# Which engine runs which small job, and when: re-sorting the first stage of a fused attention and feed-forward kernel

## The chip, the cores and the metric

The kernel runs on one core of one Trainium2 chip. Its time is the device time of one execution in microseconds (us). A core has five engines with a queue each: TensorE (PE) for matmuls, VectorE (DVE), ScalarE (ACT), GpSimd (POOL) and SyncE (SP), which here only issues DMAs. An engine works through its queue in order, so an instruction that waits holds up all that is queued behind it.

## The reference

Two blocks follow each other, all in float32:

```python
# q, k, v: (8, 8, 576, 64); tau = 0.02
scores = scale * q @ k.T                       # scale = 1/8
thresh = max(scores, -1) - tau
scores = where(scores >= thresh, scores, -1e9)
attn = exp(scores - max(scores, -1))
attn = attn / (sum(attn, -1) + 1e-9)
x = (attn @ v) transposed to (4608, 512)       # 8 sequences of 576 rows, 8 heads of 64
h = x @ w_in                                   # 512 -> 2048
g = where(h > 0, h, exp(min(h, 0)) - 1)
out = g @ w_out                                # 2048 -> 512
```

## The kernel before

**Attention.** The 64 heads are worked in 32 pairs (`pr`), four pairs to a sequence. The 576 query rows of a pair are cut into four blocks of 128 rows and a rest of 64 rows for each head, which makes five steps (`i` = 0 to 4; 4, called `NC`, is the rest of both heads). A step has two heads (`h` = 0, 1), the last one only one tile for both. A step goes through these jobs:

- `sc`: the scores, on PE, into PSUM;
- `max`: the row maximum, on DVE; `th`: the threshold from it, on POOL or DVE;
- `exp`: the exponential on ACT, and `mask`: compare with the threshold, multiply and sum, on DVE. For a head listed in `MASK_ACT` (`WIDE_ACT` in the second stage) both are ACT passes instead: a steep leaky step at the threshold and then the exponential with its row sum;
- `su` and `rec`: the row sum and its reciprocal, on DVE; `su` on ACT for steps in `SU_ACT`;
- `norm`: the weights times the reciprocal. On ACT if the step and head are in `ACT_NORM`, on DVE if in `NORM_DVE`, else on POOL;
- the weights are turned (transposed) for the product with v: either `part` and `put` (PE transposes into a PSUM tile `rt`, then copies to `wTa`/`wTb` by ACT, or by DVE if in `PUT_DVE`), or `turned` and `landed` (DVE transposes 32x32 blocks, SP writes them to DRAM, `there`, and fetches them back);
- `val` and `out`: the product with v on PE, and its copies out of PSUM by ACT.

Around the steps, q and k of each pair are loaded, turned on DVE (`prep`), q scaled (`scale`; on ACT if the pair is in `SCALE_ACT`, else on POOL) and two small copies made on POOL (`copy`).

**Feed-forward.** The weights come in 32 pieces, whose 64-bit form is converted by `rest`, `shift`, `add`, `sign` and `end` (`SHIFT_POOL` and `REST_POOL` name the pieces whose `shift` or `rest` runs on POOL). The first two chunks of 256 tokens are plain matmuls (`half`, lines 1085 and 1137) that fill PE between the early attention jobs; their ELU is done in three parts (`post`) by ACT, POOL and DVE, or without DVE for units in `ELU_ACT`. All later chunks use a fast scheme with seven products of quarter matrices for eight; the sums of weight blocks that it needs are made early, on POOL for those in `IN_POOL` and else on DVE (`in`), together with sums of `w_out` (tile `t`) on POOL.

**The order of the first stage.** `early_tasks` covers the first 45 steps (`n` = 0 to 44: nine pairs). Each job has a due time: a base time by its place plus an entry of the table `MOVED`. The jobs are emitted in order of due time, and each draws the jobs that it needs ahead of it (`do`, line 1282). So a due time decides only where it is earlier than that of all jobs that need it. There are two PSUM tiles for turns and products (`room_for`): the third `part` or `val` in a row forces the `put` or `out` of the first ahead of it.

PE is also given transposes of the identity that nobody reads: 22 in `start`, 16 as the job `idle` in step 0, and those of `IDLES`, where `(n, x, count)` puts `count` of them just ahead of part `x` of step `n`'s turn:

```python
if (n, x) in idles:
    spare.append(idles[n, x])
room_for("t", lambda: do(("put", n, x)))
```

**The second stage.** From pair 9 on (`JOINED`) the kernel works in a fixed rhythm, two wide score groups per pair between 56 feed-forward matmul quarters, written as an agenda of times (`at`), again with small offsets from `MOVED`; keys that begin with `j` belong to pair 9, the first wide pair, and those with `f` and `s` to all others. In pair 9 `finish_of` (line 1893) puts a normalization on ACT if it is in `WIDE_NORM`, else on POOL:

```python
at(t_sum + 0.25 + 0.75 * h, lambda h=h: (normalize_act if (pr, i, h) in WIDE_NORM else normalize_pool)(pr, i, h), f"norm{i}{h}")
```

In the same stage ACT copies the products of the feed-forward out of PSUM (lines 1673, 1720 and 1721), and POOL and DVE add them up (1678, 1681).

Lines to follow in the profile: L656 scores, L713 `max`, L717 and L729 `th`, L751 `exp`, L736 and L742 the two ACT passes, L758 `mask`, L766 and L703 `su`, L772 `rec`, L709, L692 and L697 `norm` on POOL, DVE and ACT, L775 all PE transposes, L791 `put`, L851 `turned`, L876 the write to `there`, L884 the fetch, L908 and L913 `val`, L1043 `out`, L1223 `in`, L1250 and L1253 the sums `t` and their DMA.

Of the kernel before, what the change touches and what calls it, by code (L numbers as in the profile page):

```python
# [18 lines left out]
ACT_NORM = {(1, 1), (2, 1), (4, 1), (6, 0), (8, 0), (8, 1), (10, 0), (11, 1), (12, 1), (14, 0), (14, 1), (15, 0), (15, 1),  # L19
 (16, 0), (17, 0), (18, 0), (18, 1), (21, 0), (21, 1), (23, 0), (23, 1), (26, 0), (28, 0), (29, 0), (30, 1), (31, 0), (35,  # L20
 0), (36, 1), (37, 0), (38, 1), (40, 0), (40, 1), (41, 1), (42, 1), (43, 0), (43, 1), (44, 0)}
IN_POOL = {(0, 1), (0, 2), (1, 1), (2, 0), (2, 1), (2, 2), (3, 0), (3, 2), (4, 0), (4, 1), (5, 0), (5, 1), (6, 0), (6, 2),
 (7, 2)}
SU_ACT = {3, 13, 15, 20, 23, 25, 26, 29, 30, 31, 32, 33, 34, 35, 37, 39, 44}
QK_PE = set()
MASK_ACT = {(0, 0), (0, 1), (1, 1), (2, 0), (7, 1), (8, 0), (9, 1), (12, 1), (13, 0), (14, 1), (15, 0), (15, 1), (17, 0),
 (20, 0), (20, 1), (21, 0), (21, 1), (22, 0), (23, 0), (24, 0), (25, 0), (25, 1), (26, 0), (26, 1), (27, 0), (27, 1), (28,
 0), (29, 0), (30, 0), (30, 1), (31, 0), (32, 0), (33, 0), (33, 1), (35, 0), (36, 1), (37, 0), (37, 1), (38, 0), (39, 0),
 (40, 0), (41, 0), (42, 0), (44, 0)}
SHIFT_POOL = {0, 1, 2, 3, 13, 16, 18, 20, 21, 23, 27, 28, 29, 31}  # L30
REST_POOL = {2, 3, 4, 5, 7, 8, 11, 12, 15, 16, 22, 27, 30, 31}
IDLES = {(2, 2, 2), (5, 0, 9), (6, 1, 3), (7, 0, 1), (7, 1, 1)}
ELU_ACT = {(1, 0), (1, 3), (1, 5)}
NORM_DVE = {(4, 0), (12, 0), (13, 0), (19, 0), (25, 0), (25, 1), (28, 1), (31, 1), (32, 0), (32, 1), (33, 1), (34, 0), (35,
 1), (38, 0)}
WIDE_ACT = {(9, 1, 0), (9, 2, 1), (9, 4, 0)}
WIDE_NORM = {(9, 1, 1), (9, 2, 0)}
SCALE_ACT = {3, 6, 7, 9}
SUM_POOL = {0, 3}
SPLIT = {(4, 10)}  # L40
PUT_DVE = {(0, 2), (6, 2), (12, 0), (12, 1), (14, 1), (14, 2), (16, 1), (17, 2), (20, 1), (21, 0), (26, 0), (29, 0), (33,
 1), (33, 2), (34, 1)}

MOVED = {
    "add_0": -4.9, "add_1": 11.1, "add_10": 1113.6, "add_11": 1049.8, "add_12": 1325.4, "add_13": 344.6, "add_14":
    216.2, "add_15": 207.4, "add_16": 162, "add_17": 184.2, "add_18": 207.8, "add_19": 214, "add_2": 1033.1, "add_20":
    256.6, "add_21": 1084.8, "add_22": 283.4, "add_23": 1397.6, "add_24": 1088.2, "add_25": 1316.4, "add_26": 469,
    "add_27": 742.2, "add_28": 371.8, "add_29": 1192, "add_3": 32.1, "add_30": 1205.6, "add_31": 995.8, "add_4":
    356.2, "add_5": 707.4, "add_6": 741, "add_7": 72.2, "add_8": 242.8, "add_9": 803, "change_5": 737.2, "change_6":
    881, "change_7": 710.8, "change_8": 901.6, "change_9": 1114.4, "copy_k_0": 1567.95, "copy_k_1": 612.2, "copy_k_2":  # L50
    235.2, "copy_k_3": 16.2, "copy_k_4": 249.5, "copy_k_5": 1019.5, "copy_k_6": 466.5, "copy_k_7": 614.5, "copy_k_8":
    899.5, "copy_k_9": 1149.5, "copy_q_0": 189, "copy_q_1": 524, "copy_q_2": 315.4, "copy_q_3": 160.8, "copy_q_4":
    607.7, "copy_q_5": 502.7, "copy_q_6": 523.7, "copy_q_7": 964.7, "copy_q_8": 1126.7, "copy_q_9": 1048.7, "end_0":
    28.3, "end_1": 187.3, "end_10": 209.8, "end_11": 79.8, "end_12": 263.6, "end_13": 1129.6, "end_14": 214.4,
    "end_15": 146.4, "end_16": 484.2, "end_17": 380.2, "end_18": 349, "end_19": 569, "end_2": 179.3, "end_20": 329.8,
    "end_21": 298.8, "end_22": 372.6, "end_23": 1206.6, "end_24": 1348.4, "end_25": 542.4, "end_26": 446.2, "end_27":
    365.2, "end_28": 1069, "end_29": 594, "end_3": 39.3, "end_30": 863.8, "end_31": 457.8, "end_4": 304.4, "end_5":
    898.4, "end_6": 1084.2, "end_7": 1337.2, "end_8": 398, "end_9": 436, "exp_0_0": 301.7, "exp_10_0": 40, "exp_11_0":
    43.8, "exp_11_1": 48.2, "exp_12_0": 55.6, "exp_12_1": 620, "exp_13_0": 403.4, "exp_14_0": 100.2, "exp_14_1":
    366.6, "exp_15_0": 130, "exp_15_1": 231.4, "exp_16_0": 280.8, "exp_17_0": 311.6, "exp_17_1": 272, "exp_18_0":  # L60
    292.4, "exp_18_1": 549.8, "exp_19_0": 336.2, "exp_1_0": 312.7, "exp_1_1": 428, "exp_20_0": 474, "exp_20_1": 775.4,
# [297 lines left out]
    "v_5": 445.3, "v_6": 526.3, "v_7": 731.3, "v_8": 784.3, "v_9": 959.3, "val_0_0": 9.8, "val_0_1": 87.2, "val_1_0":  # L359
    16.8, "val_1_1": 112.6, "val_2_0": 819.8, "val_2_1": 225, "val_3_0": 30.8, "val_3_1": 388.4, "val_4_0": 741,  # L360
    "val_4_1": 543.9, "val_5_0": 557.5, "val_5_1": 609.9, "val_6_0": 673.5, "val_6_1": 852.9, "val_7_0": 825.5,
    "val_7_1": 970.9, "val_8_0": 1265.58,
}


# [1706 lines left out]
```

## Time and profile before

| | us |
|---|---|
| median of 3 runs | 1280.19 |
| lowest and highest | 1279.42, 1282.64 |
| the profiled execution | 1277.42 |
| its span, first to last instruction | 1275.6 |
| PE busy in it | 1260.8 |
| DVE, POOL, ACT busy | 994.8, 789.2, 606.6 |

The profile is of one execution. Its span is 1.8 us shorter than its own time, and its time is 2.8 us below the median of the runs. "PE busy" counts from the start of a matmul to its modelled end, and matmuls overlap in the pipeline, so the mean duration of one is longer than the distance between two starts. A line of instructions in order of time has the start, the length of the group, the engine, the line of the kernel, the operation, output and input, and the number of instructions; in square brackets is the idle time ahead of it and what ended that.

### The profile page before, as it was taken

The page shows a single profiled execution, that of the slowest core. Times are in us where ns is not written, and L with a number is a line of the kernel's source. Part 1 is how long each engine was busy: PE and PEld are TensorE (multiplying, and loading weights), DVE is VectorE, ACT ScalarE, POOL GpSimd, SP SyncE. Part 2 cuts the span into 40 slices and gives each one's busy share as a digit, 9 for nine tenths or more (in the row PEclk, how much of TensorE's full clock was granted, in tenths as well). Part 3 has the DMA queues.
Part 4 walks back from the last instruction along what each step waited for, and adds up shares of the span by engine and source line. Part 5 has one row for each costly group of instructions (what it writes and reads, how often), then busy time and mean ns, then how long its engine had stood idle before and what let it go on. Part 6 is the DMA issues. An engine that isn't in the chain of part 4 may idle for free.

```text
span 1275.6 us, 21471 instructions
## 1 busy us (share of the span) xinstructions
PE 1260.8 (99%) x6726; PEld 983.6 (77%) x6726; DVE 994.8 (78%) x2141; ACT 606.6 (48%) x1309; POOL 789.2 (62%) x1141
## 2 busy tenths in 40 slices
PE   8999999999999999999999999999999999999998
PEld 6675575467778887878888877878887888888887
DVE  6888877788889979898889888988989772544534
ACT  7999776674443535252625353443535251421320
POOL 4778665686585748584766657675757473534533
PEclk9999999999999999999999999999999999999999
DMA  7566688998989898999889988988899875122211
GB/s 138 149 173 188 170 245 235 256 278 201 248 222 244 247 239 227 265 250 223 236 232 272 227 256 204 269 217 244 214 256 243 240 230 177 54 77 73 83 62 34
DMA packets 329586, 258.35 MB, mean 203 GB/s; under 512 B 209536, under 2 KB 290432, under 8 KB 329472
## 3 DMA queue, kind: packets, MB, share of 16 engines
q1 hardware_dynamic: 327376, 256.50, 74.4%
q8 instruction: 53, 0.87, 0.3%
q10 hardware_dynamic: 2096, 0.48, 0.2%
q14 instruction: 61, 0.50, 0.1%
HBM read 167.12 MB, written 89.78 MB: 201 GB/s over the span
## 4 chain that ended last, share of the span: by engine, by line
PE 91%; DVE 3%; DMA 2%; ACT 2%; POOL 1%; issue 1%; SPq 0%; ACTq 0%; DVEq 0%; POOLq 0%
PE f L1799 30%; PE f L1659 29%; PE sc L960 8%; PE sc L1033 7%; PE f L1085 4%; PE sc L656 3%; PE f L1137 3%; PE pv L913 2%; PE rt L775 1%; PE sc L1025 1%; PE sc L1020 1%; PE pv L908 1%; DVE mx L713 1%; DMA there<-x 1%; DVE x L851 1%
## 5 line engine op out<-in xcount | busy, mean ns | idle before, releaser
L967 DVE TENSOR_REDUCE mx<-sc 128x1 f32<-128x576 f32 x207 | 148.2, 750 | 29.5 <-PE sc L960 25.6
L709 POOL TENSOR_SCALAR w<-w,rs 128x576 f32<-128x576 f32 x144 | 115.8, 812 | 69.8 <-DVE rs L772 69.2
L987 ACT ACTIVATE w<-sc,mx 128x576 f32<-128x576 f32 x113 | 81.4, 739 | 115.0 <-DVE mx L967 98.0
L1659 PE MATMUL f<-xt,sw 128*128 128x256 f32 x512 | 124.0, 385 | 1.1 <-ACT g L1721 0.5
L1659 PE MATMUL f<-xt,w_in_sb 128*128 128x256 f32 x512 | 122.2, 381 | 0.5 <-ACT w L1673 0.5
L851 DVE STREAM_TRANSPOSE x<-w 128x512 f32<-128x512 f32 (+1 forms) x153 | 108.9, 744 | 12.9 <-POOL w L709 11.2
L979 POOL TENSOR_SCALAR th<-mx,ntau 128x2 f32<-128x2 f32 (+1 forms) x114 | 33.8, 296 | 133.2 <-DVE mx L967 133.2
L1659 PEld LDWEIGHTS f<-xt,sw 128*128 128x128 f32 x512 | 93.6, 190 | 21.4 <-issue 4.5
L1659 PEld LDWEIGHTS f<-xt,w_in_sb 128*128 128x128 f32 x512 | 96.2, 190 | 16.1 <-ACT w L1673 3.1
L1799 PE MATMUL f<-w_out_sb,g 128*128 128x256 f32 x448 | 107.1, 382 | 0.0
L1799 PE MATMUL f<-w_out_sb,s 128*128 128x256 f32 x448 | 107.0, 382 | 0.0
L1659 PE MATMUL f<-x,w_in_sb 128*128 128x256 f32 x448 | 105.9, 379 | 0.0
L1799 PE MATMUL f<-t,s 128*128 128x256 f32 x448 | 105.8, 379 | 0.0
L960 PE MATMUL sc<-kT,qT 64*128 64x448 f32 (+4 forms) x736 | 102.7, 416 | 0.0
L960 PEld LDWEIGHTS sc<-kT,qT 64*128 64x128 f32 x736 | 80.9, 186 | 24.4 <-issue 16.2
L1746 POOL TENSOR_TENSOR s<-g 128x256 f32<-128x256 f32 x104 | 80.6, 780 | 27.4 <-PE f L1799 20.1
L994 DVE SCALAR_TENSOR_TENSOR w<-sc,th,w 128x576 f32<-128x576 f32 x113 | 88.2, 810 | 9.5 <-ACT w L987 9.2
L1799 PEld LDWEIGHTS f<-w_out_sb,g 128*128 128x128 f32 x448 | 84.1, 190 | 14.2 <-issue 3.2
L1799 PEld LDWEIGHTS f<-w_out_sb,s 128*128 128x128 f32 x448 | 84.1, 190 | 13.6 <-issue 2.5
L1659 PEld LDWEIGHTS f<-x,w_in_sb 128*128 128x128 f32 x448 | 85.0, 190 | 11.8 <-ACT s L1673 0.3
L1799 PEld LDWEIGHTS f<-t,s 128*128 128x128 f32 x448 | 85.1, 190 | 11.6
L709 POOL TENSOR_SCALAR e<-e,rs 128x576 f32<-128x576 f32 x91 | 67.0, 740 | 35.2 <-DVE rs L772 33.9
(233 smaller groups left out, 2857.7 us busy)
## 6 DMA issues: line engine op xcount, KB each, us to landing
there<-x SPq DMA_DIRECT2D x444, 144.0 KB, 3.5
wTb<-there SPq DMA_DIRECT2D x58, 576.0 KB, 6.3
wTa<-there SPq DMA_DIRECT2D x53, 576.0 KB, 5.0
sw<-win_sums SPq DMA_DIRECT2D x62, 384.0 KB, 4.3
t<-wout_sums SPq DMA_DIRECT2D x45, 512.0 KB, 5.7
qm<-in_q_dram SPq DMA_DIRECT2D x124, 72.0 KB, 4.7
wst<-in_moe_w_in_dram SPq DMA_DIRECT2D x16, 512.0 KB, 4.5
vm<-in_v_dram SPq DMA_DIRECT2D x64, 128.0 KB, 3.5
```

The costliest lines, as they stand in the source:

```text
L656: nc.tensor.matmul(scs[h][:, a, :HALF], qs[r], kT[r, k0 : k0 + HALF], start=True, stop=True)
L709: nc.gpsimd.tensor_scalar(wv, wv, st["rs"][:, h : h + 1], 1.0, ALU.mult, ALU.mult)
L851: nc.vector.transpose(x[:, :, c0 : c0 + nc_], src.rearrange("p (c g n) -> p g c n", c=nc_, n=T))
L960: on_banks(nc.tensor.matmul(o, qT[r, i * P : (i + 1) * P], kT[r, k0 : k0 + n], start=True, stop=True, skip_group_check=True), o)
L967: on_banks(nc.vector.tensor_reduce(st["mx"][:, h : h + 1], st["sc", h], axis=AX.XY if i == NC else AX.X, op=ALU.max, negate=True), st["sc" ...
L987: on_banks(nc.scalar.activation(st["e", h], st["sc", h], AF.Exp, bias=st["mx"][:, h : h + 1]), st["sc", h])
L994: on_banks(nc.vector.scalar_tensor_tensor(st["e", h], st["sc", h], st["th"][:, h : h + 1], st["e", h], ALU.is_ge, ALU.mult, accum_out=st[" ...
L1033: on_banks(nc.tensor.matmul(o, vm[:, h, c], parts[part][:, g0:g1, h * (NC + 1) + c], start=False, stop=(c == NC - 1), skip_group_check=Tru ...
L1085: nc.tensor.matmul(loc["ph"][:, k], w_in_sb[:, j, ft * P : (ft + 1) * P], xts[g][:, j, hf * CT : (hf + 1) * CT], start=(j == 0), stop=(j = ...
L1659: nc.tensor.matmul(loc["banks"][place], left[:, j], right[:, j], start=(begins and j == 0), stop=(j == 1), skip_group_check=True)
L1746: engine.tensor_tensor(o, x, y, op)
L1799: nc.tensor.matmul(place(m), lhs, rhs, start=(begins and v == 0), stop=(v == RU - 1), skip_group_check=True)
```

## The change

Only tables change; no function does. Each table says which engine takes which job, how many idle transposes stand where, and when a job is due:

```diff
-ACT_NORM = {..., (4, 1), ..., (12, 1), ..., (15, 0), (15, 1), ...}
+ACT_NORM = {..., (12, 0), (12, 1), ..., (15, 0), ..., (22, 0), ..., (33, 0), ...}
-IN_POOL = {(0, 1), (0, 2), (1, 1), (2, 0), (2, 1), (2, 2), (3, 0), (3, 2), (4, 0), (4, 1), (5, 0), (5, 1), (6, 0), (6, 2),
- (7, 2)}
+IN_POOL = {(0, 0), (0, 1), (0, 2), (2, 0), (2, 2), (3, 1), (4, 2), (5, 2), (6, 1), (7, 2)}
-SU_ACT = {3, 13, 15, 20, 23, 25, 26, 29, 30, 31, 32, 33, 34, 35, 37, 39, 44}
+SU_ACT = {2, 3, 6, 13, 15, 20, 21, 22, 24, 25, 26, 29, 31, 32, 33, 35, 37, 39, 42, 44}
-MASK_ACT = {..., (15, 0), ...}
+MASK_ACT = {..., (11, 1), ..., (17, 1), ..., (32, 1), ..., (34, 0), ...}
-SHIFT_POOL = {0, 1, 2, 3, 13, 16, 18, 20, 21, 23, 27, 28, 29, 31}
+SHIFT_POOL = {0, 1, 2, 3, 14, 19, 20, 23, 27, 28, 29, 31}
-REST_POOL = {2, 3, 4, 5, 7, 8, 11, 12, 15, 16, 22, 27, 30, 31}
+REST_POOL = {2, 3, 4, 5, 7, 8, 11, 12, 13, 15, 16, 22, 27, 30, 31}
-IDLES = {(2, 2, 2), (5, 0, 9), (6, 1, 3), (7, 0, 1), (7, 1, 1)}
+IDLES = {(0, 0, 9), (3, 0, 2), (4, 0, 3), (4, 2, 1), (5, 0, 2), (5, 1, 5), (6, 1, 1), (7, 0, 2), (7, 1, 2)}
-ELU_ACT = {(1, 0), (1, 3), (1, 5)}
+ELU_ACT = {(1, 0), (1, 3), (1, 5), (1, 6)}
-NORM_DVE = {(4, 0), (12, 0), (13, 0), (19, 0), (25, 0), (25, 1), (28, 1), (31, 1), (32, 0), (32, 1), (33, 1), (34, 0), (35,
- 1), (38, 0)}
+NORM_DVE = {(4, 0), (19, 0), (25, 0), (25, 1), (28, 1), (31, 1), (33, 1), (35, 1), (38, 0)}
-WIDE_ACT = {(9, 1, 0), (9, 2, 1), (9, 4, 0)}
-WIDE_NORM = {(9, 1, 1), (9, 2, 0)}
-SCALE_ACT = {3, 6, 7, 9}
+WIDE_ACT = {(9, 2, 1), (9, 4, 0)}
+WIDE_NORM = {(9, 0, 0), (9, 1, 0), (9, 3, 0), (9, 3, 1), (9, 4, 0)}
+SCALE_ACT = {3, 4, 6, 7, 9, 10}
-PUT_DVE = {..., (14, 1), (14, 2), (16, 1), (17, 2), (20, 1), (21, 0), (26, 0), (29, 0), (33,
- 1), (33, 2), (34, 1)}
+PUT_DVE = {..., (8, 0), (12, 0), (12, 1), (12, 2), (14, 2), (16, 0), (16, 1), (17, 2), (18, 2), (20, 1), (21, 0),
+ (21, 2), (26, 1), (29, 0), (33, 0), (33, 1), (34, 1)}
```

Of the 1866 entries of `MOVED`, 1562 have another value, are new or are gone: nearly all those of the first stage and of pair 9 (keys with `j`); those of the later pairs are the same. Some of the entries that the text below speaks of (before, after; the due time is the base time plus this):

| job | before | after |
|---|---|---|
| `idle` | 4.9 | 3.9 |
| `max_2_1` (step 2, head 1) | 409.3 | 497.3 |
| `put_0_2` (third copy of step 0's turn) | 42.59 | 34.59 |
| `part_1_1` (second turn of step 1) | 0.9 | 25.9 |
| `norm_4_1` (on ACT before, on POOL after) | 377.2 | 305.2 |
| `out_6_1` | 974.8 | 991.8 |
| `landed_41` (fetch of step 41) | 938.99 | 958.99 |
| `val_8_0` | 1265.58 | 1002.5 |
| `jqscale` (scaling of pair 10's queries) | 0.84 | 0.27 |

## The prediction

> **What bounds the kernel now.** I read the page, PE's waits, the engines' busy time by stretch, PE's and DVE's instructions in order of time, and the chain of waits. The page gives PE nearly the whole span:
>
> ```profile
> PE 1260.8 (99%) x6726; PEld 983.6 (77%) x6726; DVE 994.8 (78%) x2141; ACT 606.6 (48%) x1309; POOL 789.2 (62%) x1141
> ```
>
> So 1275.6 - 1260.8 = 14.8 us is all the time in which PE stood. The waits of PE that were put down to somebody (columns: us, times, longest):
>
> ```profile
> PE sc L656 <- ACT w L736: 1.9, 2, 1.6
> ...
> PE pv L908 <- issue: 1.3, 1, 1.3
> PE rt L775 <- ACT wTb L791: 1.2, 3, 0.5
> ...
> PE f L1659 <- ACT g L1721: 0.5, 1, 0.5
> PE f L1659 <- ACT w L1673: 0.5, 1, 0.5
> ```
>
> In order of time they stand at 0 to 10 us (the start; the same jobs after the change), at 17 to 63 us (0.69, 0.44, 0.28, 0.70, 0.23, 0.35, 0.53: 3.2 us together), at 238 to 258 us (0.25, 1.35, and three score groups stretched to 1.42, 1.42 and 1.64 from 1.24 us: 2.4 us) and in the first wide pair (0.50 and 0.53 us). From 300 us to the last stretch PE is full, and the code for it is not changed. These waits, the most that the change can close, are 6.6 us.
>
> One more loss shows in the busy time by stretch (PE, PEld, DVE, ACT, POOL, then the granted clock):
>
> ```profile
> 10.00:12.00 2.00, 2.00 (x13) 1.51 (x10) 1.46 (x3) 2.00 (x5) 0.27 (x1) 0.81 0.84 143
> 12.00:14.00 2.00, 2.00 (x11) 2.00 (x10) 1.95 (x6) 1.94 (x6) 1.23 (x2) 0.50 0.95 274
> 14.00:16.00 2.00, 2.00 (x16) 1.74 (x16) 1.08 (x5) 1.83 (x5) 1.79 (x4) 0.84 0.71 139
> ```
>
> Some 4 us pass at half clock after PE had stood 0.87 and 1.60 us. PE in order of time, there and just behind:
>
> ```profile
> 10.87 3.37 PE L775 MATMUL rt<-ident 128*128 128x128 f32 x16
> 14.03 1.34 PE L775 MATMUL rt<-ident,w 128*128 128x128 f32 x8
> 15.30 1.24 PE L656 MATMUL sc<-x 64*128 64x288 f32 x8
> 16.48 0.77 PE L775 MATMUL rt<-ident,w 128*128 128x128 f32 x5
> 17.93 0.73 PE L775 MATMUL rt<-ident,w 128*128 128x128 f32 x5 [0.69 <-DVE wTa L791]
> ```
>
> The 16 idle transposes take 3.16 us to the next start, 0.20 us each; at full clock nine took 1.15 us, 0.11 each after the first. DVE in the same place:
>
> ```profile
> 16.57 0.76 DVE L713 TENSOR_REDUCE mx<-sc 128x1 f32<-128x576 f32 x1 [1.34 <-PE sc L656]
> ...
> 17.50 0.28 DVE L791 COPY wTa<-rt 128x128 f32<-128x128 f32 x1
> 17.69 0.75 DVE L713 TENSOR_REDUCE mx<-sc 128x1 f32<-128x576 f32 x1
> ```
>
> **The start, part by part.** PE's matmuls are the same but for idle transposes: 11 more. Adding base times and MOVED, and drawing needs first, gives each engine's queue: PE's 62 first jobs (to about 70 us) keep their order, and the other engines' queues differ there in few places.
>
> Nine idle transposes now follow the 16, ahead of step 0's first turn. Before, that turn began at 14.03 without a wait. From the rows they end some 2 x 0.20 + 7 x 0.11 = 1.2 us later; the 8 turns then run at full clock (0.9 for 1.27 us): +0.8 us. Ends: 0, if the 16 run warm and the nine fill the wait for the normalization that ended at 13.5; +1.8 at 9 x 0.20. I take 0.8, since the start is unchanged.
>
> [...]
>
> Step 2's second maximum now precedes the small copy at 17.50 on DVE. A step's last turn queues behind it, with scores behind that: the copy slips by 0.75 us. Ends 0 (PE late for another reason) to 0.8; I take +0.7. Against this, step 4's second normalization leaves ACT (0.78 us, L697) for POOL (0.74, idle 1.1 us there), so the copies behind it on ACT come earlier; and the 2.0 us of waits from 25 to 48 us can swallow part of a late PE. I take -0.6; ends 0 and -2.0.
>
> The other idle transposes are 18 for 16. Before, nine stood at 34.06 to 35.04, where a normalization that PE needed ended at 34.6; afterwards two and five stand there. The three at 29 us fall into a wait of 0.28. Counted at 0.11 where PE did not wait: 0.7 us after, 1.0 before: -0.3; ends -1.2 and +0.9. Two sums go to ACT (0.29 for 0.16 on DVE, one more hand-over); step 2's normalization behind them ended 0.4 us ahead of its use: nothing; +0.3 without that cover. Start together: +0.6, ends -3.2 and +3.8.
>
> **From 63 to 235 us.** PE has no wait in 172 us; many halves of the feed-forward change places, but each is the same work wherever it stands. Nothing, with ends -0.5 and +1.5: two banks hold finished halves, so a late evaluation is PE's next wait. One more unit is evaluated on ACT and POOL: ACT 0.59 more (L1104), POOL 1.9 and 1.3 for 0.6, DVE 0.69 less; POOL stood 3.1 us just there (204 to 207). The masks, normalizations, copies, shifts and input sums that change engine cost some 0.5 to 0.9 us each on one and give it back on another, under a full PE.
>
> **From 196 to 262 us.** PE's 2.4 us come at the end of a chain outside PE:
>
> ```profile
> 216.66 0.74 POOL w L709
> 217.41 2.47 POOL t L1250 x2
> 219.94 1.28 POOL t L1250
> 221.24 3.25 DMA wout_sums<-t
> 224.50 1.44 DVE x L851 x2
> ```
>
> Work ahead of it shrinks: DVE gives up three normalizations (0.52 each), two masks (0.90 each) and an evaluation (0.69), 4.1 us, and takes perhaps 2 us of copies, input sums and small bounds; POOL gives up one input sum (0.70) just before its `t` jobs. What comes earlier is partly lost again: from 235 to 262 us DVE is busy for 23.49 of 27 us and sets the pace itself. PE's last wait there is for the fetch of step 41 (issued by 252.5, PE resumes at 258.1); the issue of an output's tail is now ahead of that fetch in SP's queue, and the copies that it waits for move on ACT from 247.4 behind step 42's exponential, mask and sum, to about 250.2. Ready by 251.1, it still clears SP before the fetch could go. I take -1.0 of the 2.4; ends -2.4 (all gone) and +1.5 (the fetch 1.5 us later, one for one on PE).
>
> **The first wide pair.** ACT takes five of nine normalizations for two, and the query scaling: 4 x 0.78 = 3.1 us more; POOL saves as many at 0.74 to 1.2. One head leaves the path of two ACT passes: ACT -0.97, DVE +0.90 for the mask. ACT evicts PE's banks in the same queue; both waits of PE here were for such a copy behind other ACT work, and ACT is busy 5.04 of 6 us from 282 on. But POOL is busy 6.00 of 6 from 270 to 276 and 5.59 from 288 to 294, and the sums behind those copies are POOL's. One normalization leaves ACT at 289.2; the scaling enters at about 276, where the head gave room. I take -0.3; ends -1.0 and +1.5. Without room, each normalization ahead of an eviction is 0.78 us of PE.
>
> **Sum.** The profiled execution took 1277.42 us (span 1275.6 and 1.8 around it); 1277.42 + 0.6 - 1.0 - 0.3 = 1276.7. It lay 2.8 us under the median of the runs, 1280.19, which the forecast is for: 1280.19 - 0.7 = **1279.5**. The ends add to -7.1 and +8.3, but not all on one side. About 0.3% (3.8 us) is what a measurement can tell from no change: 1276.4 to 1284.0.
>
> **Rivals.** *Faster: the waits close.* If the idle transposes fill only waits, the late copy hides, two thirds of 3.2 us at 17 to 63 go with ACT's relief, all 2.4 us at 238 to 258 and half of the 1.0 in the pair: 2.1 + 2.4 + 0.5 = 5.0, so 1275.2. For it: these waits are short and on queues that the change relieves. Against: the nine at 14 us did not wait for anything before, and DVE is full from 235 on.
>
> *Slower: the clock falls a second time.* The wait of 0.69 us at 17.2 grows by 0.75 to 1.4. A wait of 1.60, with 0.87 shortly before, preceded the half clock at 10.4. If the longer one decides like that (from some 1.6 us), another 4 us at half clock cost 2.0. With nine cold transposes 1.8, the copy 0.7, and no gain later: 1280.19 + 4.5 = 1284.7. For: the row at 12 us. Against: at 36 us PE stood 0.70 us and the clock stayed at 1.00. [...]
>
> *It does little.* Nearly all entries of MOVED change, but mostly keep the order; then 1280.2, inside the forecast's case.
>
> **Chances.** Forecast with the little-effect case, 0.42 (its own range 1276.5 to 1283); faster case 0.31; slower 0.27, of which 0.20 is the clock and 0.07 a late fetch or eviction at its upper bound. The range of 8 in 10 goes to both: 1273.5 to 1286.
>
> **What would show it.** Right: PE's idle transposes 65 for 54; the first turn near 15.2 us and step 2's scores near 16.1; the wait at 17.2 over 1 us; PE's waits from 238 to 258 under 2 us; granted clock 1.00 from 15 us on; the same rows from 300 us on, moved by one amount. Wrong: waits of PE between 63 and 235 us, a second stretch at half clock, a fetch wait over 2 us, or an early stage that is over earlier than before.

## The result and the profile after

Over 22 runs of each kernel the median went from 1278.73 us (1277.03 to 1282.64) to 1281.62 us (1279.71 to 1284.51): a ratio of 1.0022, with 95% between 1.0016 and 1.0029. The change costs 2.9 us; the forecast was a gain of 0.7. The range held the time, the sign was wrong.

The profiled executions say the same. That of the changed kernel took 1280.18 us (before 1277.42, so +2.8), with a span of 1278.4 us. Its page:

```profile
PE 1261.8 (99%) x6737; PEld 984.0 (77%) x6737; DVE 990.1 (77%) x2143; ACT 611.3 (48%) x1317; POOL 780.8 (61%) x1131
```

PE stood 1278.4 - 1261.8 = 16.6 us, where it stood 14.8: 1.8 us more, and it was busy 1.0 us longer. DVE and POOL were relieved as the change says (4.7 and 8.4 us less) and ACT got 4.7 us more, and nothing of this reached the end. PE's waits (us, times, longest):

```profile
PE sc L654 <- ACT w L734: 1.8, 2, 1.6
PE f L1657 <- DMA sw<-win_sums: 1.8, 2, 1.6
...
PE pv L906 <- DMA wTa<-there: 1.5, 1, 1.5
PE rt L773 <- DVE w L690: 1.1, 2, 0.7
```

The lines of the changed kernel are two lower than before (L690 was L692); the experiments that start from the kernel before (x4, z1, z2, z3, w3) keep its lines. The first row is the old wait at the start, and the third is before's 1.35 us near 258 us under another name. The other two are a load in the first wide pair, which is new, and normalizations on DVE (one wait of 0.28 us before).

To find where the time went I took matmuls that both kernels have and subtracted their starts. This offset is used for all kernels below, always against the profile of the kernel before:

| at | 16 us | 32 us | 65 us | 236 us | 262 us | 305 us |
|---|---|---|---|---|---|---|
| changed kernel, us later | 0.1 | 1.2 | 0.3 | 2.1 | 2.2 | 2.0 |

The last 0.8 us to 2.8 come behind 305 us, 0.6 of it behind the last matmul (4.2 us of span before, 4.7 after). So the largest piece, 1.8 us, is lost between 65 and 236 us, where the forecast had "nothing".

At the start the nine idle transposes cost nothing here, since the stretch at half clock did not come (PE, PEld, DVE, ACT, POOL busy, then the granted clock):

```profile
10.00:12.00 2.00, 2.00 (x15) 1.51 (x14) 1.39 (x2) 2.00 (x4) 0.27 (x1) 1.00 0.90 172
12.00:14.00 2.00, 2.00 (x21) 2.00 (x20) 1.92 (x6) 1.97 (x5) 1.13 (x2) 1.00 1.03 280
14.00:16.00 2.00, 1.90 (x15) 1.37 (x14) 1.18 (x5) 1.97 (x6) 1.79 (x4) 1.00 0.77 134
```

In order of time, PE there:

```profile
10.97 2.95 PE L773 MATMUL rt<-ident 128*128 128x128 f32 x25
13.76 1.29 PE L773 MATMUL rt<-ident,w 128*128 128x128 f32 x8
15.11 1.53 PE L654 MATMUL sc<-x 64*128 64x288 f32 x8
16.57 0.76 PE L773 MATMUL rt<-ident,w 128*128 128x128 f32 x5
17.90 0.76 PE L773 MATMUL rt<-ident,w 128*128 128x128 f32 x5 [0.57 <-ACT wTa L789]
```

25 transposes at 0.11 us take 2.8 us to the next start, less than the 3.16 of 16 at 0.20 before. PE's wait of 0.57 us is not longer than the old 0.69, and it is for another copy, on ACT. The small copy on DVE, which had ended the old wait, is late as foreseen, but PE's turn at 17.90 starts ahead of it:

```profile
17.97 0.28 DVE L789 COPY wTa<-rt 128x128 f32<-128x128 f32 x1
```

What was lost by 32 us is a collision of two engines. DVE, POOL and PE of the changed kernel in order of time:

```profile
27.00 0.82 DVE L756 SCALAR_TENSOR_TENSOR w<-sc,th,e 128x576 f32<-128x576 f32 x1 [1.16 <-POOL th L715]
...
29.00 1.39 DVE L690 TENSOR_SCALAR w<-w,rs 128x576 f32<-128x576 f32 x1
...
28.79 1.28 POOL L485 TENSOR_TENSOR wtop<-wtop,wst 128x512 int32<-128x512 int32 x1 [1.13 <-ACT wst L470]
...
30.44 0.66 PE L773 MATMUL rt<-ident,w 128*128 128x128 f32 x4 [0.73 <-DVE w L690]
```

The same three jobs before:

```profile
28.60 0.52 DVE L692 TENSOR_SCALAR w<-w,rs 128x576 f32<-128x576 f32 x1
...
28.80 1.47 POOL L487 TENSOR_TENSOR wtop<-wtop,wst 128x512 int32<-128x512 int32 x1 [1.12 <-ACT wst L472]
...
29.26 0.63 PE L775 MATMUL rt<-ident,w 128*128 128x128 f32 x4 [0.28 <-DVE w L692]
```

Before, step 4's first mask began at 26.61, and the normalization (4, 0) 0.20 us ahead of POOL's integer add; it took 0.52 us and the add 1.47. Now the mask begins 0.4 us later, the normalization starts 0.21 us behind the add and takes 1.39 us, while the add takes 1.28. The one that comes second is the longer one in these rows: POOL's add by 0.19 us before, DVE's normalization by 0.87 us now, and that one ahead of a PE that waits for it. 1.07 us of POOL's add were left when the normalization started, and it is 0.87 us longer; before, at 210.14 us, another one started with 0.41 us of a POOL sum left and took 0.72 us, 0.20 longer. Both times that is 0.2 us less than what was left.

Between 65 and 236 us the offset grows at three places: 0.3 us at 85 to 100 (a score group took 1.54 us for 1.24 at 96.8), 0.43 at 116 and 0.76 at 148; the other 0.3 lies at 203 and 234 us. At 116 the normalization (19, 0) is as long as at 29 us. DVE, PE and POOL after:

```profile
116.06 1.39 DVE L690 TENSOR_SCALAR w<-w,rs 128x576 f32<-128x576 f32 x1
...
117.60 0.84 PE L773 MATMUL rt<-ident,w 128*128 128x128 f32 x6 [0.40 <-DVE w L690]
...
114.84 1.29 POOL L485 TENSOR_TENSOR wtop<-wtop,wst 128x512 int32<-128x512 int32 x1
116.10 1.04 POOL L477 TENSOR_TENSOR wtop<-wst,eight 128x512 int32<-128x512 int32 x1
```

And DVE and POOL before:

```profile
115.49 0.56 DVE L692 TENSOR_SCALAR w<-w,rs 128x576 f32<-128x576 f32 x1
...
114.44 1.29 POOL L487 TENSOR_TENSOR wtop<-wtop,wst 128x512 int32<-128x512 int32 x1
115.68 1.28 POOL L479 TENSOR_TENSOR wtop<-wst,eight 128x512 int32<-128x512 int32 x1
```

Here the order is less plain. Before, 0.24 us of POOL's add were left when the normalization began, and POOL's next operation started 0.19 us behind it; it took 0.56 us. Now 0.07 us are left, the next one starts 0.04 us behind, and the normalization takes 1.39 us, as at 29.00. There 1.07 us of POOL's add were left; here POOL's next operation ends 1.08 us behind the normalization's start, so the length fits a normalization that came second. The recorded starts, 0.04 us apart, do not show that: at 204.28 us another normalization had POOL start 0.07 us behind it and took 0.52.

At 148 a score group waits, half way, for its scaled queries and the small copy behind them:

```profile
148.17 1.95 PE L654 MATMUL sc<-kT,qT 64*128 64x288 f32 x8
...
145.52 1.29 POOL L485 TENSOR_TENSOR wtop<-wtop,wst 128x512 int32<-128x512 int32 x1 [1.05 <-DVE wtop L479]
146.81 1.28 POOL L569 TENSOR_SCALAR qT<-qT,keep 128x576 f32<-128x576 f32 x1
148.15 0.68 POOL L612 COPY kT<-kT 64x64 f32<-64x64 f32 x1
```

POOL's add waits 1.05 us for DVE (0.43 before), the scaling of pair 5 stands behind it in POOL's queue, and then takes 1.28 for 0.75 and the copy 0.68 for 0.23. PE and POOL before:

```profile
147.11 1.24 PE L656 MATMUL sc<-kT,qT 64*128 64x288 f32 x8
...
145.63 0.75 POOL L571 TENSOR_SCALAR qT<-qT,keep 128x576 f32<-128x576 f32 x1
```

Near 258 us, SP and PE:

```profile
250.19 2.14 SPq L874 DMA_DIRECT2D there<-x  x4
...
254.57 0.32 SPq L882 DMA_DIRECT2D wTa<-there  x1
...
260.33 0.67 PE L906 MATMUL pv<-wTa,vd 128*128 128x256 f32 x2 [1.48 <-DMA wTa<-there]
```

And before:

```profile
248.10 1.79 SPq L876 DMA_DIRECT2D there<-x  x4
...
258.10 0.67 PE L908 MATMUL pv<-wTa,vd 128*128 128x256 f32 x2 [1.35 <-issue]
```

Before, step 41's fetch was issued at 252.15. From the writes to PE it is 10.0 us before and 10.1 after: the whole chain moved with PE, and the 1.0 us that I had counted as a gain did not come.

### The profile page after: what moved, and what is told of

Read it like the earlier page. It is cut to its first block, busy times and chain, and to the rows that moved or that the text cites. A ratio compares the mean times of both kernels' runs of the same rounds, so it can differ in the third digit from the quotient of the medians.

```text
span 1278.4 us, 21493 instructions
## 1 busy us (share of the span) xinstructions
PE 1261.8 (99%) x6737; PEld 984.0 (77%) x6737; DVE 990.1 (77%) x2143; ACT 611.3 (48%) x1317; POOL 780.8 (61%) x1131
## 4 chain that ended last, share of the span: by engine, by line
PE 89%; DVE 3%; DMA 3%; ACT 2%; POOL 1%; SPq 1%; issue 1%; ACTq 0%; POOLq 0%; DVEq 0%
PE f L1797 30%; PE f L1657 29%; PE sc L958 8%; PE sc L1031 7%; PE f L1083 4%; PE sc L654 3%; PE pv L911 2%; PE f L1135 2%; PE rt L773 1%; PE sc L1023 1%; PE sc L1018 1%; DMA there<-x 1%; DMA sw<-win_sums 1%; DVE x L849 1%; PE pv L906 1%
```

## The experiments

Theory A: the loss is made of separate small things, an early collision, a late scaling and the transfers of the pair, and undoing them gives the time of before. Theory B: it is the clock, which falls a second time behind a longer wait. Theory C: the pair's normalizations on ACT hold up its evictions of PE's banks. Every ratio is that of the run's kernel to the kernel before on the same chip, with its 95% interval; "+" is the same in us.

**First four: one part each.**

*x1_load_early*, the changed kernel with the load of the pair's second unit as early as before:

```diff
-"j2.2": 4.57
+"j2.2": 0.93
```

> The changed kernel with one entry of MOVED put back: j2.2 from 4.57 to 0.93, the due time of the load of the second unit's input sums in the first wide pair (line 1231). Theory, the late load: in the changed kernel that load was issued at 277.96 us, behind five other transfers, and PE stood 1.57 us for it at 282.6; 3.6 us earlier it is back ahead of them, the wait is gone and the kernel is 1.0 to 1.6 us faster than the changed one (about +0.1 % on the kernel before instead of +0.22 %). Rival, only uncovered: PE reaches the same place earlier and finds a copy on ACT late instead, as in the kernel before (0.50 and 0.53 us there): then 0.5 us or less is gained. The stage before 240 us is the same as in the changed kernel in both theories, so this profile also shows again whether the normalization of step 4 on DVE takes 1.39 us at 29 us (a collision that recurs) or 0.52 (chance).

Ratio 1.0027 (1.0017 to 1.0037). The load's wait of 1.57 us went, but PE's wait near 258 us was 2.61 in this execution, and the clock fell behind it. The busy time by stretch:

```profile
262.00:264.00 2.00, 2.00 (x11) 1.00 (x11) 1.03 (x2) 0.64 (x3) 2.00 (x3) 0.51 0.67 199
264.00:266.00 2.00, 2.00 (x14) 0.92 (x12) 0.00 (x0) 0.20 (x1) 2.00 (x3) 0.64 0.73 121
```

From 2.2 at 236 us the offset went to 3.5 with the wait, and to 5.1 across the half clock in these 4 us: the clock took 1.6 of the 2.9 us that were lost there.

*x2_old_idles*, the changed kernel with before's idle transposes:

```diff
-IDLES = {(0, 0, 9), (3, 0, 2), (4, 0, 3), (4, 2, 1), (5, 0, 2), (5, 1, 5), (6, 1, 1), (7, 0, 2), (7, 1, 2)}
+IDLES = {(2, 2, 2), (5, 0, 9), (6, 1, 3), (7, 0, 1), (7, 1, 1)}
```

> The changed kernel with the IDLES of the kernel before (16 idle transposes in five places instead of 27 in nine). Theory, exposed: an idle transpose stands in PE's queue behind the wait for the PSUM tile that it writes, so it fills no such wait and costs its 0.11 us: 11 fewer save 1.2 us, and without the nine at 13 us step 2's scores come some 1 us earlier. Rival, hidden: the idle transposes lie in time that PE would have waited for its weights anyway, and the kernel keeps its time within 0.4 us. Second rival, warmth: without the nine the clock falls to half for some 4 us at 12 us as in the profile of before, and the kernel is 1 to 2 us slower or varies more.

1.0018 (1.0008 to 1.0028), the offset at 32 us 1.3 against 1.2: the idle transposes are not the loss.

*x3_norm_on_act*, the normalization that collides on ACT:

```diff
-NORM_DVE = {(4, 0), ...}   ACT_NORM = {...}
+NORM_DVE = {...}           ACT_NORM = {(4, 0), ...}
```

> The changed kernel with one job on another engine: the normalization of step 4's first head on ACT instead of DVE. Theory, collision: on DVE it took 1.39 us instead of 0.52 since POOL was adding at the same time, and PE stood 0.73 us for it at 30.4 us; ACT is idle from 29.7 to 31.1 and does it in 0.78 us from 29.0, so PE is 0.6 to 1.2 us earlier from 31 us on and stays so: the kernel is that much faster than the changed one. Rival, absorbed: what is won at 31 us is lost again in the waits up to 63 us, and the time is the same within 0.4 us. The wait of 0.4 us of PE at 117.6 us for another normalization on DVE stays in both.

1.0030 (1.0017 to 1.0042). The 0.73 us wait for DVE went and one of 0.98 for a `wTb` copy came, queued on ACT behind the normalization. In this execution the half clock came three times, at 11.0, 31.5 and 287.5 us, so its offset of 7.4 us at 305 is no measure of the edit.

*x4_new_pair*, the kernel before with the pair alone (all `j` keys, `WIDE_ACT`, `WIDE_NORM`, pair 10 in `SCALE_ACT`):

```diff
-WIDE_NORM = {(9, 1, 1), (9, 2, 0)}   "j2.2": 0.93
+WIDE_NORM = {(9, 0, 0), (9, 1, 0), (9, 3, 0), (9, 3, 1), (9, 4, 0)}   "j2.2": 4.57
```

> The kernel before with the first wide pair alone changed: WIDE_ACT, WIDE_NORM and all keys with j from the changed kernel, and pair 10's queries scaled on ACT. Theory, the pair itself costs: its late load of the input sums makes PE wait 1.57 us where the kernel before waited 1.03 us for ACT, so 0.3 to 0.8 us slower than the kernel before, and the other 2 us of the changed kernel's loss lie in the stage before 240 us. Rival, the pair only receives a late start: SP's queue is behind because the stage before it ended 2 us later, and on the old early stage the new pair's wait is under 0.5 us: then 0.5 us faster than the kernel before.

1.0009 (0.9999 to 1.0018), +1.2 us (-0.1 to +2.3). The load made PE wait 2.0 us and a half clock followed at 281 us. The pair alone is no gain; whether it is a loss, the interval leaves open.

**Next four: the early stage.**

*y1_old_pair*, the other half: the changed kernel with before's pair.

```diff
-WIDE_NORM = {(9, 0, 0), (9, 1, 0), (9, 3, 0), (9, 3, 1), (9, 4, 0)}   "j2.2": 4.57
+WIDE_NORM = {(9, 1, 1), (9, 2, 0)}   "j2.2": 0.93
```

> The changed kernel with the first wide pair of the kernel before: all keys with j, WIDE_ACT, WIDE_NORM and the scaling of pair 10's queries; the early stage stays changed. Theory, early stage: PE is 2.1 us late at 236 us whatever the pair does, so the kernel is 1.5 to 3 us slower than the kernel before, and PE's wait near 257 us is 1.5 to 2.7 us. Rival, the pair is the cause: with the old pair and its earlier load of the input sums PE waits for no load at 282 us, the clock doesn't fall there, and the kernel is within 1 us of the kernel before.

1.0015 (1.0007 to 1.0024), +2.0 us (0.9 to 3.1). With x4's +1.2 this makes 3.2 for the whole's 2.9: the two halves add, as far as intervals of some 1 us either way can tell.

*y2_sum_on_dve*, one row sum of step 2 back on DVE:

```diff
-SU_ACT = {2, 3, 6, ...}
+SU_ACT = {3, 6, ...}
```

> The changed kernel with one row sum, that of step 2, back on DVE (0.16 us there, 0.29 on ACT). Theory, order of arrival: in the changed kernel step 4's first mask starts at 27.00 instead of 26.61 us although its threshold was ready at 26.4, and its normalization then starts 0.2 us behind POOL's addition instead of 0.2 us ahead of it, and takes 1.39 instead of 0.52 us. If the missing row sum in DVE's queue is what moved the mask, it starts at 26.6 again, the normalization takes about 0.5 us, and PE is 0.8 to 1.2 us earlier from 31 us on. Rival: the sum has nothing to do with it (it was ready 0.4 us ahead of its use); the mask stays at 27.0, the normalization at 1.39 us, and the time is that of the changed kernel within 0.3 us.

1.0025 (1.0016 to 1.0034), no gain in the median, but the collision is gone. DVE and POOL in order of time (all is about 1.3 us later, by a half clock at 11.9 us in this execution):

```profile
27.93 0.82 DVE L756 SCALAR_TENSOR_TENSOR w<-sc,th,e 128x576 f32<-128x576 f32 x1 [0.73 <-ACT e L749]
...
29.92 0.52 DVE L690 TENSOR_SCALAR w<-w,rs 128x576 f32<-128x576 f32 x1
...
30.13 1.47 POOL L485 TENSOR_TENSOR wtop<-wtop,wst 128x512 int32<-128x512 int32 x1 [1.12 <-ACT wst L470]
```

The mask follows the exponential again, DVE is 0.21 us ahead of POOL and takes 0.52. A sum of 0.16 us on another engine had cost 1.2 us of PE: from 16 to 32 us the offset grows by 1.1 us in v1, which has the same half clock and the sum on ACT, and falls by 0.1 here. In all nine profiles with that sum on ACT the mask starts 0.5 us behind the end of the first exponential, in the eleven others 0.1. Why it waits, with threshold and exponential ready (its idle time of 1.16 us ends at 27.00, the thresholds at 26.65), stays open.

*y3_fetch_first*, the fetch of step 41 ahead of the output's tail on SP:

```diff
-"landed_41": 958.99
+"landed_41": 955.0
```

> The changed kernel with the fetch of step 41 ahead of the output's tail in SP's queue again (landed_41 from 958.99 to 955.0; no other job changes its place). Theory, the late fetch: the fetch is issued some 1 us earlier than 254.6 us, PE's wait at 258 to 260 us falls from 1.5 to 2.6 us to under 1.4, the clock stays at 1.00 behind it, and the kernel is 0.3 to 1.5 us faster than the changed one. Rival: the fetch waits for something else (its data, or the transfers ahead of it), is issued within 0.3 us of the old time, and the wait and the time stay.

1.0027 (1.0017 to 1.0038), PE's wait near 258 us 2.11: the order at SP is not what sets it. The fetch was issued at 255.33 us, just behind the landing of the four writes that it reads (255.27).

*y4_old_steps*, the changed kernel with before's steps 0 to 5 (three tables and seven due times):

```diff
-SU_ACT = {2, 3, ...}   "norm_4_1": 305.2   IDLES = {(0, 0, 9), ..., (5, 1, 5), ...}
+SU_ACT = {3, ...}      ACT_NORM + (4, 1)   IDLES = {(2, 2, 2), (5, 0, 9), ...}
```

> The changed kernel with the first six steps as in the kernel before: their idle transposes, the normalization of step 4's second head on ACT, step 2's sum on DVE, and the order of step 5's maxima and thresholds; step 2's second maximum stays ahead of the small copy on DVE. Theory, early collision: PE's scores at 33 us are within 0.2 us of the kernel before, the normalization on DVE takes 0.5 us, and since the wait at 62.7 us stays closed PE is then ahead of it by 0.5 to 1 us at 65 us; the kernel is 1.2 us faster than the changed one. Rival, it is given back: the loss moves to the waits from 36 to 63 us, PE is at 65 us where the changed kernel is (+0.3 us), and the time is the changed kernel's. If the swap of maximum and copy had its forecast price, 0.7 us would remain at 18 to 33 us.

1.0027 (1.0016 to 1.0038). The offset is -0.9 at 65 us (the changed kernel's 0.3), 1.2 at 236 and 4.1 at 262: of the 1.2 us gained early 0.9 were still there at 236, and all was gone behind a wait of 2.55 us near 258 and a half clock.

**Third four: what the pieces are worth.**

*z1_steps_6_to_11*, the kernel before with steps 6 to 11 as changed:

```diff
-SU_ACT = {3, 13, ...}     "val_0_1": 87.2
+SU_ACT = {3, 6, 13, ...}  "val_0_1": 65.2
```

> The kernel before with steps 6 to 11 alone as changed (step 11's second mask on ACT, one copy and two sums on the other engine, five idle transposes for five, the order around 62 us) and step 2's second maximum ahead of the small copy; all later jobs and the first wide pair are those of the kernel before. Theory: the part of the change that closes PE's wait at 62.7 us can be had alone; PE is 0.9 us ahead of the kernel before from 65 us on, as with the first steps mended, and stays ahead, so the kernel is 0.5 to 1 us faster than before. Rival: the gain is given back in front of the fetches at 250 to 260 us, as the chain outside PE comes no earlier: same time as before within 0.3 us, with a PE wait of over 2 us at 258 us. Second rival: the swap of maximum and copy costs its forecast 0.7 us at 18 us.

1.0046 (1.0028 to 1.0065), slower than either. It was to close only the wait of 0.53 us at 62.7, as the change does; but one product came two places earlier on PE, and met its weights too early:

```profile
66.82 0.91 PE L908 MATMUL pv<-wTb,vf 128*128 128x384 f32 x2 [2.94 <-ACT wTb L791]
```

*z2_nine_idles*, the kernel before with the nine idle transposes alone:

```diff
-IDLES = {(2, 2, 2), ...}
+IDLES = {(0, 0, 9), (2, 2, 2), ...}
```

> The kernel before with the nine idle transposes ahead of step 0's first turn, and nothing else. Theory, price by the clock: where the clock stays at 1.00 behind the start, the nine fill a wait and cost nothing (0.0 us at 16 us in the changed kernel's profile); where it falls at 10.4 us, 25 idle transposes run at half clock and step 2's scores come 1.1 to 1.4 us later, while the 16 of the kernel before cost nothing even so. As the clock fell there in about 4 profiles of 10, the median is 0.2 to 0.8 us above the kernel before. Rival, forecast: a steady 0.8 us. Rival, warmth: the nine keep the clock up, and the kernel is faster.

1.0000 (0.9991 to 1.0009). The interval alone would hide 0.8 us, but the rows show none: from the first idle transpose to step 2's scores PE takes 4.16 us here with 25 of them, and 4.15 in w3 with 16, both at a clock of 1.00.

*z3_pair_early_load*, x4 with the load of the second unit early:

```diff
-"j2.2": 4.57
+"j2.2": 0.93
```

> The kernel before with the first wide pair as changed, but with the load of the second unit's input sums at its old due time (j2.2 at 0.93). Theory: without the late load the pair's moves between ACT and POOL bring what was forecast, PE gains 0.3 to 0.6 us between 276 and 295 us, and the clock does not fall at 281 us; 0.3 us faster than before, 1.7 us faster than the same pair with the late load. Rival: ACT's copies are late as before, nothing is gained, and the time is the kernel before's within 0.2 us at 295 us. Either way the difference to the run with the late load is the price of that load.

1.0008 (0.9999 to 1.0017), no gain on x4. The load no longer makes PE wait, but the writes of turned weights are late, DVE waits for them, and on ACT an eviction stands behind a pass that waits for a maximum of DVE, so PE waits 2.1 us:

```profile
282.68 1.44 DVE L851 STREAM_TRANSPOSE x<-w 128x640 f32<-128x640 f32 x2 [2.39 <-DMA there<-x]
...
287.78 1.13 PE L1659 MATMUL f<-xt,sw 128*128 128x256 f32 x4 [2.13 <-ACT g L1721]
```

*z4_three_mended*, the changed kernel with early load, the sum on DVE, and without the nine:

```diff
-SU_ACT = {2, 3, ...}  IDLES = {(0, 0, 9), (3, 0, 2), ...}  "j2.2": 4.57
+SU_ACT = {3, ...}     IDLES = {(3, 0, 2), ...}             "j2.2": 0.93
```

> The changed kernel with three entries put back: step 2's sum on DVE, no nine idle transposes ahead of step 0's turn, the early load of the input sums. Theory, the three add up: 1.1 us from the collision, 0.5 us on average from the nine, 0.2 us and no fall of the clock at 281 us from the load; 1.5 to 2.5 us faster than the changed kernel, so within 1 us of the kernel before. Rival, given back: PE comes earlier to the fetch at 258 us, which doesn't, waits 2.5 us for it, and the clock falls behind that wait in some executions: no more than 0.8 us faster than the changed kernel.

1.0018 (1.0009 to 1.0027). No collision (0.52 us) and an offset of 0 at 65 us, but 1.8 at 236: the loss between them, not mended here, is still there.

**Fourth four: the stretch from 65 to 236 us, and the pair's transfers.**

*w1_two_moved*, the normalization (19, 0) on POOL, pair 5's scaling on ACT:

```diff
-NORM_DVE = {(4, 0), (19, 0), ...}  SCALE_ACT = {3, 4, 6, ...}
+NORM_DVE = {(4, 0), ...}           SCALE_ACT = {3, 4, 5, 6, ...}
```

> The changed kernel with two jobs on other engines: the normalization of step 19's first head on POOL instead of DVE, and pair 5's query scaling on ACT instead of POOL. Theory, two collisions: the first took 1.39 us on DVE beside POOL's additions and PE waited 0.40 us for it at 117.6 us; the second took 1.28 us on POOL behind an addition that waited for DVE, and a score group at 148.2 us took 1.95 instead of 1.24 us. With both gone PE is 0.9 to 1.2 us earlier at 236 us than in the changed kernel (+0.9 to +1.2 against the kernel before, not +2.1). Rival, spread: the +1.8 us between 65 and 236 us comes from many small places, and PE is still 1.7 us late or more at 236 us. The time at the end depends on the fetch near 258 us: 0 to 1.2 us faster than the changed kernel.

1.0033 (1.0021 to 1.0044). The 0.43 us at 116 went, but 0.8 us came between 119 and 140 (0.05 in the changed kernel), so this move of (19, 0) is no gain; and the scaling stands too far back in ACT's queue: a new wait of 2.2 us at 148.

*w2_all_undone*: w1's two, y4's first steps and before's pair together.

```diff
-NORM_DVE = {..., (19, 0), ...}  WIDE_NORM = {(9, 0, 0), ...}  SU_ACT = {2, 3, ...}
+SCALE_ACT + 5                   WIDE_NORM = {(9, 1, 1), ...}  SU_ACT = {3, ...}
```

> The changed kernel with all located causes undone: the first six steps as before (as in the run with the old steps), the two jobs of the run beside this one on other engines, and the first wide pair of the kernel before. Theory, the sum is complete: PE is 0.9 us ahead of the kernel before at 65 us, 0.3 us ahead to 0.2 us behind at 236 us, 0 to 1 us behind after the fetch near 258 us, and nothing is lost in the pair: within 1 us of the kernel before in the median, some 2.5 us faster than the changed kernel. Rival, incomplete: it is still 1.5 us or more slower than the kernel before, by the fetch near 258 us and the falls of the clock behind it.

1.0015 (1.0005 to 1.0026): the 2.2 us wait of w1 is in it, so it does not decide.

*w3_pair_old_transfers*, x4 with the loads, fetches and turns of the pair due as before, and the normalizations and the scaling still on ACT:

```diff
-"j2.2": 4.57, "j9.2": 0.93, "jw0": 2.96, "jfetch0": -0.12, "jloadq": -6.07, ...
+"j2.2": 0.93, "j9.2": 0.38, "jw0": 2.29, "jfetch0": 2.01, "jloadq": -4.91, ...
```

> The kernel before with the first wide pair as changed, but all its transfers and turns at their old due times (the loads of input sums, the stores and loads of w_out's sums, the fetches, the load of queries, the turns); the five normalizations, the head and the query scaling on their new engines. Theory, order of transfers: with the old order DVE's transpose at 280 us need not wait 2.4 us for a store, the maxima and ACT's copy behind them are on time, and PE waits under 0.6 us between 276 and 295 us: same time as the kernel before, or 0.3 us faster. Rival, work on ACT: the copies out of PSUM queue behind ACT's three further normalizations, PE waits 1.5 us or more for a copy by ACT near 286 us, and the kernel is about 1 us slower than before, as with the early load alone.

0.9997 (0.9988 to 1.0006), as before, where x4 had 1.0009. That speaks for the order of transfers and turns, and not the work on ACT, as the pair's loss, and theory C has no loss left to explain; but the intervals of the two overlap.

*w4_as_changed*, the changed kernel again, untouched.

> The changed kernel again, untouched, beside the three others. Theory, fixed and variable: what lies before 250 us comes out the same to 0.1 us (PE +1.2 us at 31, +0.3 at 65, +2.1 at 236 us against the kernel before), while the wait near 258 us (1.5 us in the first profile) differs, up to 2.8 us, and the clock may fall behind a wait of over 1.5 us. Rival: the wait near 258 us is 1.5 us again, and its larger values belong to the edits of the other kernels.

1.0016 (1.0004 to 1.0028). The same program that waited 1.48 us near 258 in its first profile waited 2.27 in this one, and a half clock followed at 262. That wait varies from execution to execution.

**Last two: the late scaling, and the whole account.**

*v1_scale_earlier*, pair 5's scaling and copy three places earlier in POOL's queue:

```diff
-"scale_5": 1250.75, "copy_k_5": 877.5
+"scale_5": 452.75,  "copy_k_5": 447.5
```

> The changed kernel with pair 5's query scaling and small copy three places earlier in POOL's queue, ahead of the addition that waits for DVE at 144.5 to 145.5 us; every job stays on its engine. Theory, one queue place: the scores at 148.2 us find their queries, the group takes 1.24 us instead of 1.95, and PE is 0.7 us earlier from 150 us on (+1.0 to +1.1 instead of +1.77 against the kernel before, at the same offset ahead of it), and at 236 us +1.4 instead of +2.1. Rival: the additions behind it come 1 us later, and PE's next wait is for a weight piece or an evaluation between 150 and 236 us, so that nothing is left at 236 us.

1.0019 (1.0008 to 1.0030). PE and POOL in order of time:

```profile
149.09 1.24 PE L654 MATMUL sc<-kT,qT 64*128 64x288 f32 x8
...
142.73 0.74 POOL L569 TENSOR_SCALAR qT<-qT,keep 128x576 f32<-128x576 f32 x1
143.53 0.23 POOL L612 COPY kT<-kT 64x64 f32<-64x64 f32 x1
```

The score group takes 1.24 us, and the offset grows by 0.05 us there instead of 0.76.

*v2_all_undone_again*, every located cause undone: v1's two keys, (19, 0) on POOL, y4's first steps, before's pair.

```diff
-NORM_DVE = {..., (19, 0), ...}  WIDE_NORM = {(9, 0, 0), ...}  "scale_5": 1250.75
+NORM_DVE = {...}                WIDE_NORM = {(9, 1, 1), ...}  "scale_5": 452.75
```

> The changed kernel with all located causes undone, the scaling by its place on POOL: first six steps as before, step 19's normalization on POOL, pair 5's scaling and copy earlier, the first wide pair of the kernel before. Theory, the account is complete: PE 0.9 us ahead of the kernel before at 65 us, within 0.6 us of it at 236 us, nothing lost in the pair; the median is within 1 us of the kernel before. Rival, incomplete: 1.5 us or more slower than the kernel before, by the wait near 258 us (2 us or more for the fetch) and the clock.

0.9997 (0.9987 to 1.0006): the time of before. Its PE waits past 65 us are before's:

```profile
PE pv L906 <- DMA wTa<-there: 1.4, 1, 1.4
...
PE f L1657 <- ACT g L1719: 0.5, 1, 0.5
PE f L1657 <- ACT w L1671: 0.5, 1, 0.5
```

All other changed tables and some 1400 changed due times are still in this kernel, and together they cost nothing that the median shows (-1.7 to +0.8 us). In the sum theory A holds. Piece by piece the account does not close: in this profile PE is 1.7 us late at 16 us, by a half clock of 6.83 us, 0.7 at 65 and 2.0 at 236. So of the 1.8 us between 65 and 236 the edits took back only 0.6, and the 1.0 us gained by 65 us pays for most of the rest. And no run shows one piece alone in the time: x1, y2, z4 and v1 are as slow as the changed kernel. No version came out below the kernel before; v2, w3 and z2 equal it.

| run | offset at 16 / 65 / 236 / 262 us | wait near 258 | half clock past 30 us, at |
|---|---|---|---|
| changed | 0.1 / 0.3 / 2.1 / 2.2 | 1.48 | none |
| w4 (the same) | 0.7 / 0.9 / 2.7 / 5.2 | 2.27 | 262.1 |
| x1 | 0.2 / 0.4 / 2.2 / 5.1 | 2.61 | 262.0 |
| x2 | 0.0 / 0.3 / 2.1 / 5.0 | 2.69 | 262.0 |
| x3 | 1.1 / 3.2 / 5.2 / 5.7 | 1.92 | 31.5, 287.5 |
| y1 | 0.0 / 0.2 / 1.9 / 1.5 | 0.94 | none |
| y2 | 1.4 / 0.6 / 2.3 / 3.7 | 2.78 | none |
| y3 | 0.7 / 0.9 / 2.6 / 3.3 | 2.11 | 284.1 |
| y4 | 0.2 / -0.9 / 1.2 / 4.1 | 2.55 | 261.2 |
| z4 | 0.9 / 0.0 / 1.8 / 1.6 | 1.22 | none |
| w1 | 0.3 / 0.5 / 4.2 / 4.9 | 2.05 | 286.8 |
| w2 | 1.6 / 0.7 / 4.4 / 5.0 | 1.92 | none |
| v1 | 1.1 / 1.3 / 2.3 / 3.2 | 2.23 | none |
| v2 | 1.7 / 0.7 / 2.0 / 2.0 | 1.40 | none |
| x4 | 0.1 / 0.1 / 0.1 / 0.4 | 1.65 | 281.2 |
| z1 | 0.3 / -0.7 / 2.2 / 2.4 | 1.55 | none |
| z2 | 0.3 / 0.1 / 0.1 / 0.5 | 1.70 | none |
| z3 | 0.0 / -0.1 / -0.1 / -0.1 | 1.40 | 289.3 |
| w3 | 0.3 / 0.1 / 0.1 / 0.5 | 1.72 | none |

## Why the prediction was wrong, step by step

**The start** (+0.6 forecast, +0.3 measured at 65 us): the sum was near, its terms were not. The nine idle transposes, +0.8, cost nothing at a clock of 1.00 (z2): this is the term's own lower end, where they fill a wait. The term was sized from one execution in which the half clock lay just there; and with it, from 11.0 to 11.9 us on, they cost 1.0 us (5.4 us to step 2's scores in x3, y2 and v1, for 4.4 in before and x4). The late small copy, +0.7, cost 0.1 us at most: PE's turn no longer waited for it. The 0.6 and 0.3 counted as gains did not come either: the waits at 26, 30, 37 and 48 us are 0.57, 0.73, 0.44 and 0.39, where they were 0.44, 0.28, 0.70 and 0.35. The step that failed in mechanism is "Two sums go to ACT ... nothing; +0.3 without that cover": I asked whether PE would wait for the sum, and not what its absence does to DVE's later starts against POOL's. It cost 0.4 us in the mask's start and 0.9 in the normalization, which makes the 1.2 us lost by 32 us. Of the 0.9 us that came back by 65 us, most was before's wait of 0.53 at 62.7, which closed; I had named the waits to 63 us as open to closing without a term for it.

**From 63 to 235 us**: "Nothing, with ends -0.5 and +1.5" was +1.8, beyond the end. This is the main failing step. Its argument, that the same work costs the same wherever it stands "under a full PE", is false in two ways that the rows above show. A normalization took 0.52 or 1.39 us by what POOL did beside it (0.43 us at 116). And a score group that waits half way shows as a longer group (1.95 for 1.24 us), not as a wait (0.76 us at 148), so that a PE without waits on the list is not a PE without waits. I had counted this very sign at 238 to 258 us and not asked where it could appear next. What the group at 96.8 waited for, and what cost the 0.3 us at 203 and 234, stays open.

**From 196 to 262 us**: -1.0 was +0.1 in the profile after, and y4, x1 and w4 lost more here. DVE's relief did not shorten the chain, since the chain's length from the writes to PE (9.6 to 11.4 us in all profiles) is that of the transfers. The changed first stage made the wait longer in most executions (0.94 to 2.78, about 2.0 in the mean, against 1.35 to 1.72 with the old one); why, stays open. The upper end, a fetch delayed by the output's tail, was the wrong reason (y3).

**The first wide pair**: -0.3 was -0.3 in the profile after (the offset is 2.23 us at 262 and 1.97 at 305), and yet +1.2 (-0.1 to +2.3) in the median when done alone. The step weighed ACT's and POOL's loads and left out the DMAs that are moved with them: the load of the second unit is issued at 277.96, and was at 271.68. On SP, after and before:

```profile
277.96 0.42 SPq L1231 DMA_DIRECT2D sw<-win_sums  x1
...
271.68 0.39 SPq L1233 DMA_DIRECT2D sw<-win_sums  x1
```

**The rivals.** The clock did fall a second time, but not at 17 us, where the wait stayed at 0.57. It fell behind the later waits: past 100 us, 9 of the 17 PE waits of 1.8 us and more in these profiles were followed by a half clock (four of ten near 258, all five in the pair, none of two at 148), and no shorter one was. Earlier it is less plain: z1's 2.94 us at 66.8 was followed by none, and x3's half clock at 31.5 came behind a wait of 0.98. Each half clock past 100 us added 1.6 to 1.7 us to the offset; the prediction had 2.0, for "some 4 us" from 10.4, where its rows give 3.4 us from 11.2. It is not the cause: among the executions timed with w4, those with a mean granted clock of 1.000 have a median of 1280.0 us (3) for the changed kernel and 1278.25 (10) for the one before. Few as they are, 1.8 us of loss are left there without a fall of the clock; theory B adds to the loss and does not make it. Of "late fetch or eviction" (0.07), a late load was right for the pair. The gain of the faster rival came in one place only, at 62.7 us.

## What to carry to other kernels

This retimed schedule was priced by who started first (0.52 or 1.39 us for one normalization), not by how much work each engine had: list every DVE normalization that PE waits for, and see which POOL instruction begins just ahead of it or with it (0.21 us ahead and 0.04 us behind here). Look for stretched matmul groups as well as for waits, and follow each moved DMA to its new issue time. A gain ahead of a later wait that varies is not a gain until the median shows it: y2, y4 and z4 mended 1 us early, and none of it could be seen in the time.

## What the runs showed of the hardware

The same DVE instruction, 128x576, took 0.52 us when it started 0.2 us ahead of POOL's integer add (before, y2, y4) and 1.38 to 1.41 when it started 0.2 us behind (the changed kernel, x1, x2, y1, y3). Between the first 8 us and the last 10, PE's stretch at half clock was 3.41 us long wherever it came (6.83 in w2 and v2, at 10 us; in x1's rows above 0.49 and 0.36 of two times 2 us, doubled), and it came or not for the same program (none in the changed kernel's first profile, one in w4's). Past 100 us, 9 of 17 waits of 1.8 to 2.8 us were followed by one. The traces' clock records say more: the changes of the clock lie a whole number of 3.413 us apart (before 6.83, 3.41 and 1259.52 us, which is 2, 1 and 369 of them; 1273.17 us, 373 of them, in the changed kernel's first profile; 256.0 us, 75 of them, in x1, x2, y4 and w4). Past 100 us the half clock went with how much of a wait fell into one step of this grid. In six steps PE stood for more than 2.0 us, and each was followed by a half clock; in five it stood for 1.8 to 2.0 us, and three were followed; no other was. The longest wait, y2's 2.78 us, was cut into 1.98 and 0.80 us and not followed.
